# A kernel of three blocks with its whole order written as a list: a new list, filler products early in it, and one reciprocal for both softmaxes

## The chip, the core and the metric

The kernel runs on one core of a Trainium2 chip. The metric is the time of one execution on the device in microseconds. The profile of one execution shows the engines of the core: PE (TensorE, its weight loads as PEld), DVE (VectorE), ACT (ScalarE), POOL (GpSimd) and SP (SyncE), which issues the DMAs.

## The reference, cut to what matters

Attention with a band and a pooled part, then a convolution block on its result, then a mixer with two low-rank factors and two more products. q, k and v are float32; all weights are float64.

```python
def _attn_ref(q, k, v):                       # 4 batches, 8 heads, 576 tokens, 64 channels
    a = exp(s - max(s)); a = a / (sum(a) + 1e-9)          # both softmaxes
    q_d, k_d, v_d = means over 4 neighbouring tokens
    out_up = repeat(sm_attn(q_d, k_d, v_d), 4)            # 144 x 144 scores a head
    mask = |i - j| < 4                                    # the local part
    return out_up + attn_local @ v
def _moe_ref(x, w_in, conv_w, w_out):         # 512 -> 1024 -> 512
    h = relu(x @ w_in); conv of 3 taps over tokens; gate = sigmoid(conv_out)
    return h * gate @ w_out
def _moe2_ref(x, U, V, w_ch1, w_ch2):         # rank 32 over 576 tokens; 512 -> 2048 -> 512
    u = x + (x^T @ U @ V)^T
    return u + relu(u @ w_ch1) @ w_ch2
```

## The kernel before, in words

The order of everything is one string, SEQ, of 2671 words. A word is a step and its indices (`S.0.2`: scores of pair 0 in PSUM slot a2); the last lines of the kernel look each word up in a table and call its function, and a step's instructions go to the engines' queues in that order. Each engine works its queue in order, and semaphores hold it where data or a buffer is not there yet. So the list sets, for each engine, who stands behind whom.

Attention works on 16 pairs of heads, four to a batch. Steps of pair p, with engine and line:

- `lq`, `lw`, `lr` load q and k, the v windows, and v (SP, L273, L278, L282). `qs` sums four neighbours of q and k (DVE, L287); `qd` puts the scaled q sums into blocks (ACT, L295).
- `S` local scores: two mask products of 192 columns with `identR` as weights (L304) and 96 small matmuls (L311) on PE. `M` negative maxima (DVE, L326), `D` the shift (DVE, L333), `E` exp (ACT, L339), `R` row sums (DVE, L343).
- `Sd` pooled scores (PE, L364), `Md` maxima (DVE, L369), `Ed` three exps with sums (ACT, L376).
- `re`, `r` add eps (ACT, L348) and take the reciprocal (DVE, L352) of the 12 local sums; `rde`, `rd` do so for the three pooled sums. `n`, `nd` multiply (POOL, L357, L381; `nv`, `ndv` on DVE).
- `T`, `Td` transposes on PE (L398, L405); `c`, `cd` copy them from PSUM (ACT; `cv`, `cdv` on DVE); `V` 96 small matmuls with v (PE, L425), `Vd` the pooled ones (PE, L433), `vs` sums of v (POOL, L388, L391; `vsv` on DVE); `xd` scales (ACT, L441; `xdv` on DVE) and `x` adds into X (DVE, L452).

Weights come as 64-bit words. `wl` loads a tile (SP, L472; `lc` the conv weights); `wd.*.0` takes the upper words as float (ACT, L482); `wd.*.1` to `wd.*.3` shift and fill in the lower bits (DVE, L484, L486, L489; `cw.0` to `cw.3` do it for the conv weights); `wh` rounds to the first part (ACT, L502) and `wo` takes the rest (POOL, L505; `wO` on DVE). There are 16 tiles of group 1 and 32 of group 2.

The products work on six blocks of 384 tokens. Block 0 needs pairs 0 to 3, block 1 pairs 0 to 7. `px`, `pl` split X in two parts (ACT and POOL). `1.n.c` is the first product (PE, L618), n = 8 x block + tile of d_ff; `r1`, `c0`, `c1`, `th`, `gm`, `gh`, `gl` are ReLU, the conv taps, tanh, the gate (DVE, L656) and its two parts; `2.n.c` is the second product (L672). Then come the mixer (`mh` to `ma`), the turned result (`u`) and the products 3 (L746) and 4 (L764). `%Z` hands the PSUM slots 1 and 2 of attention to the products, `%A` and `%M` free SBUF of attention and of the mixer. `sp` are products on zeros ahead of the first data.

Of the kernel before, what the change touches and what calls it, by code (L numbers as in the profile page):

```python
# [18 lines left out]
SEQ = ("sf xz k z sp.1 uz lq.0 lr.0 lq.1 sp.0 lr.1 lq.2 lw.0 K lw.1 sp.1 lw.2 wl.1.0 lc wl.1.1 qs.0 wl.1.2 S.0.2 vs.0.0 "  # L19
# [164 lines left out]
P = 128  # L184
# [5 lines left out]
def mixer_kernel(ctx, tc, consts, qk, vw_, vr_, w1, w2, cw_, u_, v_, out):  # L190
# [57 lines left out]
    def clear():  # L248
        nc.gpsimd.memset(eps, 1e-9)
        for t in qds:  # L250
            nc.gpsimd.memset(t, 0.0)

    def spin_fill():
        t = pools["spin"] = xu.tile([P, 512], F32, name="spin", tag="xu0")
        nc.vector.memset(t, 0.0)
# [612 lines left out]
```

## Time and profile before

| what | value |
|---|---|
| time, median of 3 | 765.02 us (764.52 to 765.95) |
| the profiled execution | 764.64 us, span 762.7 us |
| busy in the span | PE 736.5, PEld 652.8, DVE 397.6, ACT 298.7, POOL 172.3 us |
| mean granted clock of PE | 0.975 of full |
| matmuls | 6634 |
| DMA | 46.72 MB read, 4.72 MB written |

The time is that of the whole execution; the span runs from the first instruction to the last. Busy times of PE are from instructions whose ends are modelled, so a busy PE is not one at its peak. The clock has two levels, 1.2 and 2.4 GHz; a mean between them is a mix in time.

### The profile page before, as it was taken

The numbers are of one execution on the slowest core, as the hardware profiler recorded it, in microseconds if no ns is written. First come the engines' busy times: TensorE is split into PE (matmuls) and PEld (weight loads), VectorE is DVE, ScalarE is ACT, GpSimd is POOL, SyncE is SP. The second block draws the span as 40 slices with busy tenths as digits, with TensorE's granted clock in tenths as the row PEclk, the third lists the DMA queues.
The fourth block names the chain that finished last, engine by engine and source line by source line (L and its number), as shares of the span: only waits on it lengthen the run. The fifth ranks groups of instructions, "written<-read, shape, count | busy, mean of one in ns | idle before, by whom it ended". The sixth has DMA issues, their size and how long they took to land.

```text
span 762.7 us, 15404 instructions
## 1 busy us (share of the span) xinstructions
PE 736.5 (97%) x6634; PEld 652.8 (86%) x6634; DVE 397.6 (52%) x661; ACT 298.7 (39%) x682; POOL 172.3 (23%) x161
## 2 busy tenths in 40 slices
PE   6997899999999999999999999999999999999998
PEld 4876788889988888888889898999899898988996
DVE  6479999775764899798986211311121131112111
ACT  5467686554754776665353111211111121111110
POOL 4355654652231546243221000000000000000000
PEclk9569999999999999999999999999999999999999
DMA  9854742211102200353240100100010010001001
GB/s 316 252 188 137 247 160 80 76 48 38 55 2 89 80 0 29 111 170 134 78 199 0 42 1 1 41 1 1 1 42 0 1 42 1 0 1 42 1 0 42
DMA packets 16388, 52.43 MB, mean 69 GB/s; under 512 B 1984, under 2 KB 2496, under 8 KB 16320
## 3 DMA queue, kind: packets, MB, share of 16 engines
q1 hardware_dynamic: 16320, 51.44, 19.8%
q8 instruction: 52, 0.85, 0.5%
q14 instruction: 16, 0.13, 0.1%
HBM read 46.72 MB, written 4.72 MB: 67 GB/s over the span
## 4 chain that ended last, share of the span: by engine, by line
PE 83%; DVE 11%; issue 2%; ACT 1%; DMA 1%; SPq 0%; POOL 0%; DVEq 0%; POOLq 0%; ACTq 0%
PE g L746 25%; PE acc L764 25%; PE g L618 10%; PE acc L672 10%; PE O L425 3%; DVE wval L486 2%; DVE wval L489 2%; PE Sd L364 2%; PE S L311 2%; PE O L433 1%; DVE g L645 1%; DVE wval L484 1%; PE Td L405 1%; DVE ss L287 1%; PE h L696 1%
## 5 line engine op out<-in xcount | busy, mean ns | idle before, releaser
L746 PE MATMUL g<-uT,w 128*128 128x384 f32 x1152 | 214.2, 338 | 0.9 <-DVE a L755 0.9
L764 PE MATMUL acc<-w,a 128*128 128x512 f32 x864 | 211.1, 395 | 0.2 <-DVE a L755 0.2
L746 PEld LDWEIGHTS g<-uT,w 128*128 128x128 f32 x1152 | 202.3, 188 | 7.2 <-DVE a L755 2.7
L764 PEld LDWEIGHTS acc<-w,a 128*128 128x128 f32 x864 | 161.1, 188 | 33.5 <-DVE a L755 0.7
L755 DVE SCALAR_TENSOR_TENSOR a<-g,a 128x384 fp32r<-128x384 f32 x96 | 53.4, 556 | 250.4 <-ACT a L751 250.2
L751 ACT ACTIVATE a<-g 128x384 fp32r<-128x384 f32 x96 | 47.1, 490 | 275.5 <-PE g L746 169.9
L618 PE MATMUL g<-xhl,w 128*128 128x386 f32 (+1 forms) x576 | 117.3, 349 | 3.0 <-POOL w L505 1.7
L672 PE MATMUL acc<-w,ghl 128*128 128x512 f32 x432 | 110.5, 398 | 0.5 <-POOL ghl L664 0.5
L618 PEld LDWEIGHTS g<-xhl,w 128*128 128x128 f32 x576 | 103.2, 193 | 8.9 <-POOL w L505 2.5
L672 PEld LDWEIGHTS acc<-w,ghl 128*128 128x128 f32 x432 | 79.7, 188 | 17.2 <-POOL ghl L664 0.9
L664 POOL TENSOR_TENSOR ghl<-ct,ghl 128x384 fp32r<-128x384 f32 x48 | 53.0, 1105 | 94.7 <-ACT ghl L661 89.1
L645 DVE SCALAR_TENSOR_TENSOR g<-h,cw,g 128x384 f32<-128x384 f32 x96 | 59.3, 619 | 27.6 <-ACT g L640 26.0
L505 POOL TENSOR_TENSOR w<-wval,w 128x512 fp32r<-128x512 f32 x31 | 42.7, 1379 | 77.5 <-ACT w L502 73.2
L502 ACT ACTIVATE w<-wval 128x512 fp32r<-128x512 f32 x48 | 30.1, 630 | 40.5 <-DVE wval L489 40.2
L486 DVE SCALAR_TENSOR_TENSOR wval<-raw,wval 128x512 uint32<-128x512 uint32 x48 | 43.1, 898 | 1.3
L489 DVE SCALAR_TENSOR_TENSOR wval<-raw,wval 128x512 uint32<-128x512 uint32 x48 | 42.5, 889 | 1.1
L425 PEld LDWEIGHTS O<-PT,vw 32*64 32x64 f32 x1536 | 27.5, 148 | 7.8 <-issue 5.7
L425 PE MATMUL O<-PT,vw 32*64 32x24 f32 x1536 | 29.4, 223 | 4.0 <-issue 3.1
L624 ACT ACTIVATE h<-g 128x386 f32<-128x386 f32 (+1 forms) x48 | 23.5, 490 | 22.4 <-PE g L618 22.0
L482 ACT ACTIVATE wval<-raw 128x512 f32<-128x512 f32 x48 | 31.1, 663 | 1.5 <-DVE w L505 1.0
L661 ACT ACTIVATE ghl<-ct 128x384 fp32r<-128x384 f32 x48 | 24.9, 521 | 14.0 <-PE acc L672 6.8
L656 DVE SCALAR_TENSOR_TENSOR ct<-g,h 128x384 f32<-128x384 f32 x48 | 26.4, 550 | 6.8 <-POOL ghl L664 3.4
(88 smaller groups left out, 641.0 us busy)
## 6 DMA issues: line engine op xcount, KB each, us to landing
raw<-in_w_dram SPq DMA_DIRECT2D x48, 512.0 KB, 5.4
qk<-in_qk_dram SPq DMA_DIRECT2D x16, 576.0 KB, 8.1
vw<-in_vw_dram SPq DMA_DIRECT2D x16, 384.0 KB, 3.5
vr<-in_vr_dram SPq DMA_DIRECT2D x16, 288.0 KB
out_dram<-u SPq DMA_DIRECT2D x17, 256.0 KB, 2.1
uvr<-in_v_dram SPq DMA_DIRECT2D x1, 576.0 KB
uvr<-in_u_dram SPq DMA_DIRECT2D x1, 320.0 KB
out_dram<-u SPq DMA_DIRECT2D x2, 128.0 KB, 2.0
```

Source lines behind the costliest of these rows:

```text
L425: nc.tensor.matmul(o[D * h:D * h + D, jh, c:c + NQ], e["vw"][32 * s:32 * s + 32, t, a], e["PT"][32 * s:32 * s + 32, t, 32 * a:32 * a + NQ] ...
L486: nc.vector.scalar_tensor_tensor(out=d, in0=lo, scalar=29, in1=d, op0=ALU.logical_shift_right, op1=ALU.bitwise_or)
L489: nc.vector.scalar_tensor_tensor(out=d, in0=hi, scalar=0x80000000, in1=d, op0=ALU.bitwise_and, op1=ALU.bitwise_or)
L505: eng.tensor_tensor(W[k][:, 1], vals.pop(k), W[k][:, 0].bitcast(F32), op=ALU.subtract)
L618: nc.tensor.matmul(gp[n][:, :wd], w[:, a, cc], xhl[g, cc][:, b, :wd], start=cc == 0 and i == 0, stop=cc == NCC - 1 and i == 2)
L645: nc.vector.scalar_tensor_tensor(out=o, in0=inner(g, hts[n], k), scalar=cw[:, k * NF + f:k * NF + f + 1], in1=o, op0=ALU.mult, op1=ALU.add)
L664: eng.tensor_tensor(ghl[n][:, 1], cts.pop(n), ghl[n][:, 0].bitcast(F32), op=ALU.subtract)
L672: nc.tensor.matmul(acc[g][c], t[:, a, c * P:(c + 1) * P], w[:, b], start=f == 0 and i == 0, stop=f == NF - 1 and i == 2)
L746: nc.tensor.matmul(gp["3", m][:, :TB], w[:, a, cc], uT[g, cc][:, b, :TB], start=cc == 0 and i == 0, stop=cc == NCC - 1 and i == 2)
L751: nc.scalar.activation(out=t[:, 0], in_=gp["3", m][:, :TB], func=AF.Relu)
L755: nc.vector.scalar_tensor_tensor(out=t[:, 1], in0=gp.pop(("3", m))[:, :TB], scalar=0.0, in1=t[:, 0].bitcast(F32), op0=ALU.max, op1=ALU.sub ...
L764: nc.tensor.matmul(acc2[g][c], t[:, a, c * P:(c + 1) * P], w[:, b], start=f == 0 and i == 0, stop=f == NF2 - 1 and i == 2)
```

## The change

Most of the diff is SEQ: the new list has 2643 words and all steps of the old one except `rde` and `rd`. Of the others some have another PSUM slot, and some went from POOL to DVE, from DVE to ACT or the other way (`wo` and `wO`, `ml` and `mL`, and so on). Three things are new in the code. `f.n` (three words: `f.9`, `f.6`, `f.1`) issues n products of the constants `identR` and `mask`, 192 columns each, into columns 320 to 511 of the PSUM tile that was last taken in an a slot; nothing reads them. `wm` runs an exp on the eps tile on ACT. The sums of both softmaxes lie in one of three fixed tiles of 15 columns, set to one at the start, and `re` and `r` work on all 15 columns and 128 partitions at once.

The heads of both lists, up to the line with the first product step `1.0.0`:

```diff
--- before.py
+++ after.py
-SEQ = ("sf xz k z sp.1 uz lq.0 lr.0 lq.1 sp.0 lr.1 lq.2 lw.0 K lw.1 sp.1 lw.2 wl.1.0 lc wl.1.1 qs.0 wl.1.2 S.0.2 vs.0.0 "
-       "qd.0 M.0 lq.3 Sd.0.1 vs.0.1 D.0 S.1.1 qs.1 E.0 lr.2 vs.1.0 Md.0 qd.1 lq.4 R.0 Ed.0 Sd.1.0 vs.1.1 M.1 lr.3 D.1 "
-       "Md.1 rde.0 re.0 E.1 r.0 rd.0 n.0 qs.2 Ed.1 nd.0 T.0.1 S.2.2 R.1 rde.1 c.0 rd.1 nd.1 Td.0.1 re.1 M.2 lq.5 qd.2 "
-       "V.0.0 r.1 D.2 cd.0 n.1 cw.0 E.2 cw.1 T.1.1 cw.2 cw.3 lw.3 Vd.0 wd.1.0.0 R.2 Td.1.2 c.1 wd.1.0.1 wl.1.3 wd.1.0.2 "
-       "Sd.2.0 xd.0 cd.1 x.0 V.1.1 re.2 wd.1.1.0 Md.2 px.0.0 wl.1.4 wd.1.1.1 Vd.1 Ed.2 wd.1.1.2 lw.4 r.2 pl.0.0 S.3.2 "
-       "qs.3 xd.1 n.2 rde.2 wd.1.2.0 x.1 lq.6 vs.2.0 T.2.1 qd.3 wl.1.5 M.3 px.0.1 Sd.3.0 D.3 vs.2.1 rd.2 E.3 S.4.0 cv.2 "
-       "nd.2 lr.4 Md.3 vs.3.0 V.2.2 R.3 Ed.3 M.4 D.4 vs.3.1 Td.2.1 qs.4 lw.5 rde.3 pl.0.1 re.3 lr.5 E.4 cd.2 rd.3 lq.7 "
-       "r.3 nd.3 qd.4 Vd.2 qs.5 Sd.4.0 n.3 xd.2 x.2 qd.5 T.3.1 Td.3.1 wd.1.2.1 c.3 S.5.0 wd.1.1.3 px.0.2 cd.3 Md.4 "
-       "pl.0.2 V.3.2 wh.1.1 R.4 lq.8 wd.1.2.2 Ed.4 wd.1.0.3 Vd.3 lw.6 M.5 wo.1.1 xd.3 Sd.5.0 D.5 re.4 rde.4 wh.1.0 x.3 "
-       "E.5 wo.1.0 r.4 %Z rd.4 px.0.3 Md.5 R.5 Ed.5 nd.4 1.0.0 qs.6 1.0.1 n.4 1.0.2 wd.1.3.0 vsv.4.0 T.4.0 Td.4.0 re.5 "
...
+SEQ = ("sf xz k z lq.0 uz wm lw.0 sp.1 lr.0 lq.1 lw.1 lr.1 sp.0 K lq.2 lw.2 lc wl.1.0 sp.1 wl.1.1 qs.0 wl.1.2 S.0.2 qd.0 "
+       "vs.0.0 Sd.0.1 M.0 lq.3 D.0 vs.0.1 Md.0 E.0 f.9 S.1.2 lr.2 R.0 Ed.0 qs.1 re.0 vs.1.0 r.0 qd.1 lq.4 M.1 f.6 Sd.1.1 "
+       "D.1 n.0 E.1 qs.2 nd.0 R.1 cw.0 qd.2 vsv.1.1 T.0.0 cw.1 lr.3 cw.2 Md.1 Td.0.2 wd.1.0.0 cw.3 c.0 wd.1.0.1 wl.1.3 "
+       "S.2.1 wd.1.0.2 cd.0 Ed.1 wd.1.0.3 re.1 wh.1.0 r.1 V.0.2 M.2 lq.5 n.1 wd.1.1.0 D.2 nd.1 wd.1.2.0 wl.1.4 E.2 "
+       "wl.1.5 qs.3 wo.1.0 vs.2.0 R.2 qd.3 T.1.1 lw.3 Td.1.1 c.1 wd.1.1.1 wd.1.1.2 V.1.0 wd.1.1.3 wd.1.2.1 wh.1.1 "
+       "wd.1.2.2 wd.1.2.3 wd.1.3.0 vs.3.0 wh.1.2 wl.1.6 wd.1.3.1 wd.1.3.2 Vd.0 lw.4 wd.1.3.3 wo.1.1 wh.1.3 Sd.2.1 cd.1 "
+       "wo.1.3 xd.0 Vd.1 wd.1.4.0 x.0 wl.1.7 Md.2 px.0.0 vs.2.1 S.3.2 qs.4 Ed.2 pl.0.0 lr.4 re.2 vs.3.1 xd.1 r.2 qd.4 "
+       "x.1 n.2 lr.5 Sd.3.1 lq.6 M.3 px.0.1 nd.2 D.3 E.3 wd.1.4.1 T.2.0 Md.3 pl.0.1 Td.2.2 c.2 R.3 Ed.3 wo.1.2 qs.5 "
+       "V.2.1 re.3 vs.5.0 cd.2 r.3 qd.5 wd.1.4.2 wd.1.5.0 wd.1.4.3 Vd.2 wd.1.6.0 wl.1.8 lw.5 wd.1.5.1 wh.1.4 wl.1.9 "
+       "wd.1.5.2 S.4.0 xd.2 wd.1.5.3 x.2 nd.3 wh.1.5 px.0.2 wd.1.6.1 wd.1.6.2 Sd.4.0 lq.7 M.4 n.3 D.4 wo.1.5 f.1 T.3.1 "
+       "Md.4 E.4 Td.3.2 R.4 Ed.4 vs.4.0 qs.6 S.5.0 cd.3 vs.4.1 c.3 qd.6 wd.1.6.3 lr.6 re.4 pl.0.2 wh.1.6 r.4 V.3.2 M.5 "
+       "lq.8 nd.4 D.5 E.5 Vd.3 nv.4 lw.6 Sd.5.0 R.5 wo.1.4 xd.3 x.3 vs.5.1 wd.1.7.0 %Z 1.0.0 Md.5 px.0.3 vs.6.0 wl.1.10 "
...
```

The rest of the diff:

```diff
@@ -229,6 +227,7 @@
     mask = pa.tile([P, 6, NW], F32R, name="mask")
     eps = const.tile([P, 1], F32, name="eps")
     qds = [pa.tile([P, 3, 96], F32, name=f"qd{i}") for i in range(2)]
+    sms = [pa.tile([P, 15], F32, name=f"sm{i}") for i in range(3)]
     cw = const.tile([P, NK * NF], F32, name="cw")
 
     def load_consts():
@@ -247,8 +246,14 @@
 
     def clear():
         nc.gpsimd.memset(eps, 1e-9)
+        for t in sms:
+            nc.gpsimd.memset(t, 1.0)
         for t in qds:
             nc.gpsimd.memset(t, 0.0)
+
+    def warm():
+        t = const.tile([P, 1], F32, name="warm")
+        nc.scalar.activation(out=t, in_=eps, func=AF.Exp)
 
     def spin_fill():
         t = pools["spin"] = xu.tile([P, 512], F32, name="spin", tag="xu0")
@@ -260,10 +265,18 @@
 
     st = {}
     for p in range(NPAIR):
-        st[p] = {}
+        st[p] = {"p": p}
+
+    last = {}
 
     def slot_a(n, name):
-        return (ps0 if n < 1 else pst).tile([P, 2, 512], F32, name=name, tag=f"a{n}")
+        t = last["a"] = (ps0 if n < 1 else pst).tile([P, 2, 512], F32, name=name, tag=f"a{n}")
+        return t
+
+    def beat(n):
+
+        for _ in range(n):
+            nc.tensor.matmul(last["a"][:, 1, 320:512], identR, mask.rearrange("p j x -> p (j x)"), start=True, stop=True)
 
     def slot_b(n, name):
         return (ps0 if n < 1 else pst).tile([P, 512], F32, name=name, tag=f"b{n}")
@@ -315,7 +328,7 @@
     def stats(e):
         if "sm" not in e:
             e["nm"] = pa.tile([P, 15], F32, name="nm", tag="nm", bufs=3)
-            e["sm"] = pa.tile([P, 15], F32, name="sm", tag="sm", bufs=3)
+            e["sm"] = sms[e["p"] % 3]
 
     def view(s):
         return s[:, :, :6 * NW].rearrange("p h (j x) -> p h j x", j=6)
@@ -775,10 +788,9 @@
     A, V = nc.scalar.copy, nc.vector.tensor_copy
     DV, GP = nc.vector, nc.gpsimd
     ACTS = {
-        "k": load_consts, "K": make_consts, "xz": x_pads, "z": clear, "sf": spin_fill, "sp": spin,
+        "k": load_consts, "K": make_consts, "xz": x_pads, "z": clear, "sf": spin_fill, "sp": spin, "f": beat, "wm": warm,
         "lq": load_qk, "lw": load_vw, "lr": load_vr, "qs": sums, "qd": q_blocks, "S": scores, "M": maxima,
-        "D": shifted, "E": exps, "R": rowsums, "re": lambda p: eps_add(p, P, 0, 12), "r": lambda p: recip(p, P, 0, 12),
-        "rde": lambda p: eps_add(p, 96, 12, 15), "rd": lambda p: recip(p, 96, 12, 15),
+        "D": shifted, "E": exps, "R": rowsums, "re": lambda p: eps_add(p, P, 0, 15), "r": lambda p: recip(p, P, 0, 15),
         "n": lambda p: norm(p, GP), "nv": lambda p: norm(p, DV),
         "Sd": scores_d, "Md": maxima_d, "Ed": exps_d, "nd": lambda p: norm_d(p, GP), "ndv": lambda p: norm_d(p, DV),
         "vs": vsum, "vsv": lambda p, i: vsum(p, i, DV), "T": trans, "Td": trans_d, "c": lambda p: copy_T(p, A), "cv": lambda p: copy_T(p, V),
```

## Rows read from the trace of the kernel before

**Rows 1.** Stretches of the span: busy us (instructions) of each engine, PE clock, DMA share, GB/s
```profile
0.00:51.40 51.40, 42.38 (x1081) 34.80 (x1082) 30.18 (x56) 24.76 (x79) 21.04 (x29) 0.72 0.80 259
51.40:119.90 68.50, 58.15 (x1128) 49.78 (x1127) 65.98 (x103) 50.22 (x130) 41.05 (x37) 0.93 0.53 177
119.90:250.00 130.10, 130.09 (x1888) 115.93 (x1889) 90.08 (x163) 74.94 (x184) 49.19 (x48) 1.00 0.18 56
250.00:400.00 150.00, 146.96 (x722) 128.80 (x721) 133.99 (x207) 95.16 (x184) 58.32 (x46) 1.00 0.27 98
```

**Rows 2.** Timeline of PE: start us, us, instructions [idle before <-releaser]
```profile
20.09 2.12 PE L425 MATMUL O<-PT,vw 32*64 32x24 f32 x69 [3.11 <-issue]
...
46.29 2.77 PE L425 MATMUL O<-PT,vw 32*64 32x24 f32 x96
...
98.82 1.59 PE L425 MATMUL O<-PT,vw 32*64 32x24 f32 x96
...
102.43 2.36 PE L618 MATMUL g<-xhl,w 128*128 128x386 f32 x12
...
119.91 0.43 PE L304 MATMUL S<-mask,identR 128*128 128x192 f32 x2 [1.47 <-DVE X L452]
```

**Rows 3.** DMA from 17.5 to 18 us: queue, packets, MB, share of 16 engines
```profile
q8 instruction: 1, 0.02, 12.8%
```

**Rows 4.** Timeline of DVE, first data and the step x.0
```profile
5.73 1.35 DVE L287 TENSOR_REDUCE ss<-qk 128x288 f32<-128x1152 f32 x1 [2.00 <-DMA qk<-in_qk_dram]
...
24.59 0.76 DVE L452 TENSOR_TENSOR X<-O,xd 128x576 f32<-128x576 f32 x1 [4.79 <-ACT xd L441]
```

**Rows 5.** Timeline of ACT (ScalarE), table load and conv weights
```profile
7.16 1.28 ACT L295 ACT_TABLE_LOAD   x1 [7.16 <-DVE ss L287]
...
17.41 0.22 ACT L482 ACTIVATE cw<-craw 128x24 f32<-128x24 f32 x1 [0.32 <-DMA craw<-in_cw_dram]
```

**Rows 6.** Groups by line and shape: count | busy us, mean ns | idle before, releasers
```profile
L486 DVE SCALAR_TENSOR_TENSOR wval<-raw,wval 128x512 uint32<-128x512 uint32 x48 | 43.1, 898 | 1.3
...
L489 DVE SCALAR_TENSOR_TENSOR wval<-raw,wval 128x512 uint32<-128x512 uint32 x48 | 42.5, 889 | 1.1
...
L656 DVE SCALAR_TENSOR_TENSOR ct<-g,h 128x384 f32<-128x384 f32 x48 | 26.4, 550 | 6.8 <-POOL ghl L664 3.4 <-ACT g L649 3.3
...
L484 DVE TENSOR_SCALAR wval<-wval 128x512 uint32<-128x512 uint32 x48 | 24.3, 512 | 1.5 <-ACT wval L482 1.5
...
L287 DVE TENSOR_REDUCE ss<-qk 128x288 f32<-128x1152 f32 x16 | 21.3, 1331 | 2.4 <-DMA qk<-in_qk_dram 2.0 <-PE Sd L364 0.4
...
L376 ACT ACTIVATE Pd<-Sd,nm 96x144 f32<-96x144 f32 x48 | 17.5, 369 | 2.4 <-DVE nm L369 2.3
...
L452 DVE TENSOR_TENSOR X<-O,xd 128x576 f32<-128x576 f32 x16 | 12.1, 756 | 11.7 <-ACT xd L441 11.4
L505 DVE TENSOR_TENSOR w<-wval,w 128x512 fp32r<-128x512 f32 x17 | 12.1, 711 | 1.0 <-ACT w L502 1.0
...
L369 DVE TENSOR_REDUCE nm<-Sd 96x3 f32<-96x432 f32 x16 | 9.5, 597 | 2.5 <-PE Sd L364 2.4
...
L333 DVE TENSOR_TENSOR P<-S,nm 128x384 f32<-128x384 f32 x16 | 8.9, 556 | 1.2 <-DVE nm L326 0.5
...
L343 DVE TENSOR_REDUCE sm<-P 128x12 f32<-128x384 f32 x16 | 8.6, 536 | 0.2
...
L304 PE MATMUL S<-mask,identR 128*128 128x192 f32 x32 | 8.1, 338 | 2.3 <-DVE X L452 2.3
...
L388 DVE TENSOR_TENSOR vr<-vr 72x512 f32<-72x512 f32 x5 | 5.4, 1086 | 0.0
...
L352 DVE RECIPROCAL sm<-sm 128x12 f32<-128x12 f32 x16 | 3.4, 214 | 0.0
...
L352 DVE RECIPROCAL sm<-sm 96x3 f32<-96x3 f32 x16 | 2.4, 152 | 1.2 <-ACT sm L348 1.2
...
L357 DVE TENSOR_TENSOR P<-P,sm 128x384 f32<-128x384 f32 x3 | 1.6, 549 | 0.0
```

304 rows, old and new, of the table SEQ are left out of this document.

## Prediction

> **What bounds the kernel now.** I read the stretches of the span first [rows 1], because they show where the tensor engine (PE) loses time. From 119.9 us to 250 us it is never idle at the full clock; from 250 to 400 it loses 3.0 us. Ahead of 119.9 us it is idle for 51.4 - 42.38 = 9.0 and 68.5 - 58.15 = 10.35 us, and its granted clock is 0.72 and 0.93 of full, that is, the 1.2 GHz level for about 0.28 x 51.4 x 2 = 29 and 0.07 x 68.5 x 2 = 10 us. At half speed that costs up to 19 us more. So up to 39 us lie in the first 120, and the change has to earn its gain there.
>
> Which engine rules that part? The same rows answer for DVE: it works 30.18 of the first 51.4 us (21.2 idle) and 65.98 of the next 68.5 (2.5 idle). The boundary is the end of x.3, the last step that block 0 of the products needs from attention. Thus there are two stages. In the first nobody is full and everybody waits in chains; in the second DVE is full, and PE's last wait of it, at 119.91, is for a DVE step [rows 2]. After it PE is full.
>
> The PE rows show what the first stage does [rows 2]: after part of V.0, PE stands 3.11 us on "issue", waiting for no other engine, and then V takes 2.77 us where it takes 1.59 us at the full clock. The instruction queue moved a block of 0.02 MB at 17.5 us, in the middle of that stand [rows 3], when the data loads held the DMA engines; I take it for PE's program that came late. On DVE the same event is an idle time of 4.79 us ahead of x.0 [rows 4].
>
> **Part by part.** *The list up to x.3.* Counting the words of both lists up to x.3, the new one has on DVE four more each of the decode steps 1 and 2 and five more of step 3, one more each of qs, R, r and the norm, and four small reciprocals fewer. With the rows of each [rows 6]: 4 x 0.512 + 4 x 0.898 + 5 x 0.889 = 10.1; 1.33 + 0.54 + 0.21 + 0.55 = 2.6; less 4 x 0.152 = 0.6: 12.1 us more. (The weight tiles decoded by then go from two to seven.) DVE's work up to x.3 becomes 30.2 + 12.1 = 42.3 us.
>
> When is x.3 done? I add the idle time that I cannot see filled. DVE gets its first data at 5.73 us [rows 4]; nearly all time before is idle, 4.8 us. Decoding cannot start until the conv weights and the first weight tile have landed; the conv weights came at 17.4 us [rows 5], and ScalarE decodes in order. The new list asks for them one 512 KB tile earlier, but for the first weight tile, which is needed next, one small load later, so I leave 17.4. From 5.7 to there the new list offers DVE three qs at 1.33, two each of M, D, R and Md at about 0.56, and about 1.1 us of small steps [rows 6], 9.6 us in all: 2.1 us idle. Then decode steps stand between the dependent ones, and I allow 1 us a pair for what is not covered (x.0 waits behind cd.1 and three hi-parts on ScalarE), 4 us. So 42.3 + 4.8 + 2.1 + 4 = 53.2 us, against 51.4 before. Bounds: 49 with no waits for pairs, 58 if PE at half clock paces the pairs again (V at 2.77 us, and so with its other small matmuls, is what made the old chain).
>
> *From x.3 to the point where PE is full.* I compare equal PE work. Before, that point is step S.10 at 119.9. The new list has the same PE work ahead of step 1.8.0 (15 matmuls of the first product more, 12 of which take 2.36 us [rows 2], and the fillers; V at 1.59 us and five smaller steps of one pair fewer; I set the rest at 0.5 us less). DVE has less to do by then: one D, Md, R and x (0.556 + 0.597 + 0.536 + 0.756), two v sums and two low parts that went to POOL (2 x 1.086 + 2 x 0.711) and nine small reciprocals (9 x 0.152) are gone, 7.4 us; one gate, one decode step 1, one step 2 and one norm are added, 2.5 us [rows 6]. Net 4.9 us less: 30.18 + 65.98 - 4.9 = 91.3 us. Between x.3 and 1.8.0 that leaves 49 us of DVE work. At the old idle rate of 2.5 in 66 it would idle 1.9 us; since the new order runs PE and DVE side by side at nearly one rate, each will wait for the other now and then, and I take 4 (1.9 to 8). So 1.8.0 comes at 53.2 + 49 + 4 = 106.2, where the old list would stand at 119.4: 13.2 us gained.
>
> *After it.* The new list brings the rest of attention forward (x.12 and x.15 stand before fewer products), so DVE stays nearly full where it had 90.1 of 130.1 us [rows 1]. PE is no longer alone in setting the pace; I give back 3 us (0 to 8). The 3.0 us of PE gaps at 250 to 400 can go or double (3 either way); I leave them. The last steps are the same.
>
> *One reciprocal.* For each pair a DVE instruction of 0.152 us goes (counted above), and one of two small ScalarE additions. In exchange r.p waits for Ed.p too. Behind it on DVE stand M, D and decode steps of the next pair, and E of that pair waits for those. The old small reciprocal waited for the same Ed through its addition, 1.2 us in all sixteen [rows 6], so I put it at nothing and keep the other end as a rival. The fixed tiles add three small memsets on POOL ahead of its first data; nothing.
>
> *Filler products.* 16 matmuls of the form of S's mask product, 0.338 us each by its row [rows 6]: 5.4 us at most. Nine stand where S.1 waits for D.0 to leave its PSUM slot, six ahead of Sd.1.1, which waits for qd.1. I count them as hidden; if the cover is gone, the 5.4 us delay M.1 and its chain, within the bounds above.
>
> *The table load.* ScalarE loads its table for 1.28 us at 7.16 [rows 5], between qs.0 and qd.0, with all of Sd.0, Md.0 and Ed.0 behind. The new activation on eps takes it to a time when nothing is there. Gain 0 to 1.3 us, inside the 2.1 us above.
>
> *Loads.* Ten weight tiles instead of six are asked for ahead of x.3, 2.1 MB on 51.4 us at 259 GB/s (13.3 MB) [rows 1]. The share of 0.80 would go to about 0.93 at equal time. They are behind the pairs' loads on SP; a late tile holds ScalarE, and DVE behind it, in the first stage.
>
> *The program's arrival.* Before V.0's stand PE had run 348 matmuls (6 fillers, S.0, S.1 and S.2 at 98, two Sd, one T, one Td, 27 of V.0). In the new list the 348th is the twelfth of V.0, but V.0 comes behind wd.1.0.0 on ScalarE and not right after S.2, so the block has time to arrive: the 3.1 us go into the 2.1 and 4 us above and not on top. The Trainium skill ("Runtime: NRT & Kernel Launch", section "Instruction fetch mechanics") says that the next 16 KiB block is fetched while the current one runs, and that dispatch is slower than the fill, so that fetching stays hidden. By it there is no such wait to remove, and the sum would be 3.1 us worse, 757.5, inside the forecast's own span. The trace does not agree: the 3.11 us stand on "issue" with the block moving in it.
>
> Sum: 13.2 - 3 = 10.2 us. The profiled execution took 764.64 us (span 762.7 and 1.9 around it), 0.4 under the median of 765.02; I predict 764.6 - 10.2 = 754.4.
>
> **Rivals.** (a) *PE's clock still paces the start, or the weight tiles come late.* For it: the old stage had 0.72 of the clock although PE was busy for 42.38 of 51.4 us in it [rows 1], and DMA stood at 0.80. Against: the added decode work needs no PE. x.3 at 58 us and 8 instead of 4 us of waits leave 764.6 - (13.2 - 4.8 - 4 - 3) = 763.2; the usual case of it, 760 to 763. The Trainium skill ("TensorE: Matmul & The Clock Gate", Part 1) says that the point where the clock changes moves from run to run of one kernel, which would undo fillers that were fitted to one trace. No trace here shows it; the three times before lie within 1.4 us, so it can hardly be worth more. (b) *Better than that:* x.3 at 49, old idle rate, nothing given back: 764.6 - (13.2 + 4.2 + 2.1) = 745.1. It needs the first stage to run without chains. (c) *No change:* the gain is real at 106 us and is lost again by 400, where DVE is at 134 of 150 us [rows 1]. Against: DVE idles 40 us between 119.9 and 250, so there is room. 765. (d) *Slower:* the joined reciprocal. r.p holds DVE until Ed.p is done, in a stage where DVE sets the pace. Three exps are 3 x 0.369 = 1.1 us [rows 6]; exposed in all pairs that is 17.7 us, against 10.2 gained: 772.1. It decides from 0.64 us a pair on. Against: the 1.2 us in all that the old one waited, and decode steps between Ed and r in the new list.
>
> **Chances.** Forecast (748 to 760) 0.57; (a) 0.15; (b) 0.10; (c) 0.06; (d) 0.12. The range 746 to 763 takes in (a) and half of (b). Three runs differ by 1.4 us, so 0.2% (1.5 us) is about what a measurement can tell from no change: faster 0.82, same 0.06, slower 0.12.
>
> **What would show it.** x.3 on DVE at 51 to 56 us with about 42 us of DVE work ahead; no stand of 3 us on "issue" in V.0; DVE at 95% from there; PE free of waits from about 106 us; waits of the reciprocal on ScalarE of a few us in all. The forecast fails if x.3 comes after 60 us, if PE keeps waiting for DVE between 110 and 170, or if new PE gaps of more than 3 us appear after 250.

## The result, and the profile after

The kernel before took 765.49 us (median of four, 764.52 to 769.50), the changed one 755.35 us (754.93 to 755.94): ratio 0.9858, with a 95% interval of 0.9822 to 0.9894. The forecast was 754.4 us. The profiled execution after took 755.43 us (span 753.7), 9.2 less than that of before. In the changed file every line of the kernel's functions stands 13 further down than the one of before (a few at the top differ): V is L438, x L465, the first product L631, the joined reciprocal L365, the fillers L279.

The stretches of the span after, in the columns of [rows 1], cut at the end of x.3 (60.6 us) and at product step 1.8.0 (113.7 us, the 13th of the 21 matmuls that start at 111.51):

```profile
0.00:60.60 60.60, 46.27 (x1097) 37.96 (x1098) 46.15 (x68) 31.32 (x88) 33.39 (x42) 0.66 0.78 259
60.60:113.70 53.10, 52.76 (x1021) 46.57 (x1020) 50.76 (x78) 40.76 (x103) 35.19 (x32) 0.97 0.49 166
113.70:250.00 136.30, 136.30 (x2020) 121.88 (x2019) 104.17 (x179) 83.95 (x201) 48.73 (x46) 1.00 0.21 67
250.00:400.00 150.00, 148.16 (x735) 131.22 (x735) 127.95 (x199) 90.69 (x175) 50.41 (x42) 1.00 0.25 92
```

DVE works 46.15 of the first 60.6 us and idles 14.45; before it worked 30.18 of 51.4 and idled 21.2 [rows 1]. The first stage is longer by 9.2 us, and DVE does 16 us more in it: seven weight tiles are decoded there instead of two. From x.3 on PE loses 0.3 us in 53 instead of 10.35 in 68.5, and after 250 us it idles 1.84 us instead of 3.04. The clock of the first stage did not rise (0.66 of full against 0.72).

PE's timeline after shows the places that [rows 2] shows of before:

```profile
13.90 0.25 PE L279 MATMUL S<-mask,identR 128*128 128x192 f32 x1 [1.13 <-issue]
...
22.04 2.54 PE L438 MATMUL O<-PT,vw 32*64 32x24 f32 x84 [2.20 <-issue]
...
29.74 1.91 PE L438 MATMUL O<-PT,vw 32*64 32x24 f32 x62 [2.18 <-issue]
...
51.93 0.53 PE L279 MATMUL S<-mask,identR 128*128 128x192 f32 x1 [3.10 <-DVE P L346]
...
55.52 2.77 PE L438 MATMUL O<-PT,vw 32*64 32x24 f32 x96
...
76.52 0.47 PE L317 MATMUL S<-mask,identR 128*128 128x192 f32 x2 [0.32 <-DVE X L465]
...
111.51 3.98 PE L631 MATMUL g<-xhl,w 128*128 128x386 f32 x21
```

Three stands on "issue", 5.5 us, take the place of one of 3.11. They come after 222, 348 and 475 matmuls, so 126 and 127 apart. Ahead of 250 us PE's last wait for DVE is at 76.5 us; before it was at 119.9. V at 55.52 still takes 2.77 us, the price of the 1.2 GHz level [rows 2].

DVE's timeline after, from its wait for the fillers to x.3:

```profile
14.19 0.56 DVE L346 TENSOR_TENSOR P<-S,nm 128x384 f32<-128x384 f32 x1 [2.28 <-PE S L279]
...
24.22 0.42 DVE L497 TENSOR_SCALAR wval<-wval 128x512 uint32<-128x512 uint32 x1
24.67 1.64 DVE L499 SCALAR_TENSOR_TENSOR wval<-raw,wval 128x512 uint32<-128x512 uint32 x1
...
27.41 0.69 DVE L499 SCALAR_TENSOR_TENSOR wval<-raw,wval 128x512 uint32<-128x512 uint32 x1
...
38.89 2.59 DVE L497 TENSOR_SCALAR wval<-wval 128x512 uint32<-128x512 uint32 x1
...
57.27 1.63 DVE L370 TENSOR_TENSOR P<-P,sm 128x384 f32<-128x384 f32 x1
...
59.84 0.76 DVE L465 TENSOR_TENSOR X<-O,xd 128x576 f32<-128x576 f32 x1 [0.48 <-ACT xd L454]
```

The same instruction takes 0.42 or 2.59 us, and 0.69 or 1.64. The groups of DVE's line and shape in the first 60.6 us give the means (count | busy us, mean ns | idle before):

```profile
L499 DVE SCALAR_TENSOR_TENSOR wval<-raw,wval 128x512 uint32<-128x512 uint32 x7 | 7.6, 1088 | 0.2
L497 DVE TENSOR_SCALAR wval<-wval 128x512 uint32<-128x512 uint32 x7 | 5.7, 821 | 1.0 <-ACT wval L495 1.0
L502 DVE SCALAR_TENSOR_TENSOR wval<-raw,wval 128x512 uint32<-128x512 uint32 x7 | 5.4, 773 | 0.2
...
L365 DVE RECIPROCAL sm<-sm 128x15 f32<-128x15 f32 x5 | 1.2, 245 | 1.9 <-ACT sm L361 1.9
```

The table load runs at once, and the conv weights land 1.4 us earlier than before [rows 5]; from ScalarE's timeline after:

```profile
0.73 1.28 ACT L256 ACT_TABLE_LOAD   x1 [0.73 <-PEq L866]
...
16.04 0.23 ACT L495 ACTIVATE cw<-craw 128x24 f32<-128x24 f32 x1 [0.73 <-DMA craw<-in_cw_dram]
```

### The profile page after: what moved, and what is told of

It is laid out like the page before. It is cut to its first block, busy times and chain, and to the rows that moved or that the text cites. A ratio compares the mean times of both kernels' runs of the same rounds, so it can differ in the third digit from the quotient of the medians.

```text
span 753.7 us, 15425 instructions
## 1 busy us (share of the span) xinstructions
PE 733.5 (97%) x6650; PEld 653.6 (87%) x6650; DVE 399.0 (53%) x647; ACT 297.2 (39%) x668; POOL 170.3 (23%) x161
## 4 chain that ended last, share of the span: by engine, by line
PE 84%; DVE 9%; DMA 3%; ACT 2%; issue 2%; SPq 0%; POOL 0%; DVEq 0%; ACTq 0%
PE g L759 26%; PE acc L777 26%; PE g L631 11%; PE acc L685 10%; PE O L438 2%; DVE wval L499 2%; DMA raw<-in_w_dram 2%; DVE wval L497 1%; PE S L324 1%; DVE wval L502 1%; DMA vr<-in_vr_dram 1%; PE Sd L377 1%; PE O L446 1%; PE ut L743 1%; DVE g L658 1%
## 5 line engine op out<-in xcount | busy, mean ns | idle before, releaser
L777 PE MATMUL acc<-w,a 128*128 128x512 f32 x864 | 208.6, 392 | 0.0
L631 PE MATMUL g<-xhl,w 128*128 128x386 f32 (+1 forms) x576 | 115.4, 347 | 1.0 <-DVE ct L669 1.0
L685 PE MATMUL acc<-w,ghl 128*128 128x512 f32 x432 | 108.3, 395 | 0.0
L631 PEld LDWEIGHTS g<-xhl,w 128*128 128x128 f32 x576 | 101.8, 191 | 6.0 <-DVE ct L669 2.3
L677 POOL TENSOR_TENSOR ghl<-ct,ghl 128x384 fp32r<-128x384 f32 x48 | 50.6, 1056 | 105.7 <-ACT ghl L674 86.1
L658 DVE SCALAR_TENSOR_TENSOR g<-h,cw,g 128x384 f32<-128x384 f32 x96 | 59.1, 619 | 27.2 <-ACT g L653 25.6
L438 PEld LDWEIGHTS O<-PT,vw 32*64 32x64 f32 x1536 | 27.9, 149 | 8.4 <-issue 7.3
L438 PE MATMUL O<-PT,vw 32*64 32x24 f32 x1536 | 29.8, 224 | 4.5 <-issue 4.4
L662 ACT ACTIVATE g<-g 128x384 f32<-128x384 f32 x48 | 22.7, 473 | 21.1 <-DVE g L658 21.0
```

The costliest lines, as they stand in the source:

```text
L438: nc.tensor.matmul(o[D * h:D * h + D, jh, c:c + NQ], e["vw"][32 * s:32 * s + 32, t, a], e["PT"][32 * s:32 * s + 32, t, 32 * a:32 * a + NQ] ...
L631: nc.tensor.matmul(gp[n][:, :wd], w[:, a, cc], xhl[g, cc][:, b, :wd], start=cc == 0 and i == 0, stop=cc == NCC - 1 and i == 2)
L658: nc.vector.scalar_tensor_tensor(out=o, in0=inner(g, hts[n], k), scalar=cw[:, k * NF + f:k * NF + f + 1], in1=o, op0=ALU.mult, op1=ALU.add)
L677: eng.tensor_tensor(ghl[n][:, 1], cts.pop(n), ghl[n][:, 0].bitcast(F32), op=ALU.subtract)
L685: nc.tensor.matmul(acc[g][c], t[:, a, c * P:(c + 1) * P], w[:, b], start=f == 0 and i == 0, stop=f == NF - 1 and i == 2)
L777: nc.tensor.matmul(acc2[g][c], t[:, a, c * P:(c + 1) * P], w[:, b], start=f == 0 and i == 0, stop=f == NF2 - 1 and i == 2)
```

## The experiments

Twelve kernels, each timed in five rounds beside the kernel before on the same chip; a ratio is to that kernel. Three questions: where in the list the gain lies, what paces the first stage before and after (DVE's work or PE's), and what the small parts are worth. A difference between two kernels is taken from their ratios, times 765 us; each ratio has an uncertainty of some 0.3%, 2 us, and a difference of two kernels with the change some 3 us.

**The new head with the old rest, and the reverse.** The cut is at step V.9.0 of the new list and step 1.10.2 of the old one, where both have done nearly the same steps. Words that come from the old list keep their two reciprocals. With NEW and OLD for the two lists of words, h1_newhead and h2_oldhead in turn:

```diff
+SEQ = NEW[:594] + [w for w in OLD if w not in NEW[:594]]
```
```diff
+SEQ = OLD[:612] + [w for w in NEW if w not in OLD[:612]]
```

> The new list up to V.9, then all that is left in the old order, with the old split reciprocals for the pairs of that part. The kernel before has done the same steps (but one product step, 0.55 us) at 136.7 us, the changed one at 132.7, so theory 1 (the first part and the rest each give about half) says 4.6 us under the kernel before: about 760.5. Theory 2, that of the prediction (all of the gain is made ahead of the stretch in which PE is full, and a little is given back after it) says 755 to 756. Theory 3 (the gain is the rest's alone) says 765.

Measured: 758.56 us (757.65 to 760.33), ratio 0.9896 [0.9875, 0.9917], 8.0 us less than before.

> The old list up to 1.10.2, with the old split reciprocals, no fillers and the table load in its old place, then all that is left in the new order. Theory 1 says 9.8 - 4.6, so about 5 us under the kernel before: 760. Theory 2 says 765, theory 3 says 755 to 756.

Measured: 764.59 us (761.88 to 767.87), ratio 0.9977 [0.9953, 1.0002], 1.8 us less, not to be told from nothing. The two add up to 9.8 of 10.9. So most of the gain goes with the head, which has `wm` in it (its price is measured below); the result lies between theories 1 and 2. With the old rest PE also waits after 250 us as it did before; from PE's timeline of h1_newhead between 250 and 400:

```profile
259.22 2.40 PE L634 MATMUL g<-xhl,w 128*128 128x388 f32 x12 [0.85 <-DVE ct L672]
...
292.58 0.74 PE L733 MATMUL mx<-Ht,Vs 128*128 128x512 f32 x2 [0.60 <-DVE Ht L721]
...
329.32 0.79 PE L634 MATMUL g<-xhl,w 128*128 128x386 f32 x3 [0.62 <-DVE ct L672]
...
369.79 2.37 PE L762 MATMUL g<-uT,w 128*128 128x384 f32 x12 [0.91 <-DVE a L771]
```

After the whole change two waits of half a microsecond or more are left there, in the same view:

```profile
258.25 1.32 PE L631 MATMUL g<-xhl,w 128*128 128x388 f32 x6 [1.01 <-DVE ct L669]
...
338.12 2.36 PE L759 MATMUL g<-uT,w 128*128 128x384 f32 x12 [0.63 <-DVE a L768]
```

The new rest of the list removes 1.2 us of PE's waits in those 150 us (3.04 to 1.84 us idle), which is of the size that h2_oldhead gave.

**The joined reciprocal, alone in the old list and taken out of the new one.**

```diff
-... Md.1 rde.0 re.0 E.1 r.0 rd.0 n.0 qs.2 Ed.1 nd.0 T.0.1 S.2.2 R.1 rde.1 c.0 rd.1 nd.1 Td.0.1 re.1 ...
+... Md.1 re.0 E.1 r.0 n.0 qs.2 Ed.1 nd.0 T.0.1 S.2.2 R.1 re.1 c.0 r.1 nd.1 Td.0.1 ...
```

> The old list with one reciprocal for both softmaxes and nothing else of the change. DVE loses 16 small reciprocals of 0.15 us, ten of them ahead of 120 us. If DVE's work sets the pace there, 1 to 2 us less: 763 to 764. If each pair now pays for the wait for Ed (1.1 us), up to 772; two pairs (10 and 13) have Ed late and their norm moved. If neither counts, 765.

Measured: 767.14 us (764.21 to 772.78), ratio 1.0005 [0.9979, 1.0031].

In s_new each `re.p` of the new list is two additions and each `r.p` two reciprocals, of 12 and of 3 columns.

> The changed kernel with the two old reciprocals and additions, side by side where the joined one stands. If DVE's and ScalarE's work sets the pace, 11 x 0.15 = 1.7 us more up to 133 us, and up to 2.4 in all: 757 to 758. If the joining is hidden, 755.4.

Measured: 756.41 us (755.85 to 756.64), ratio 0.9863 [0.9840, 0.9886], against 0.9858 of the changed kernel. Neither direction shows a price. In the old list the joined reciprocals wait 4.2 us for ScalarE's additions in all sixteen pairs (1.2 before [rows 6]), against 16 x 0.152 = 2.4 us of DVE's work that goes.

**The fillers.** f_none drops `f.9 f.6 f.1` from the new list, f_9only drops `f.6 f.1`.

> The changed kernel without the 16 filler products. Its trace shows three waits at them: D.1 waits 2.28 us for f.6, PE stands 1.13 us on issue inside f.6, and f.1 waits 3.10 us for D.4 with T.3 and V.3 behind it. If these are what the fillers do, the kernel gets 1 to 4 us faster: 752 to 754. If the fillers hold the clock up and so shorten the start, it gets 1 to 5 us slower: 756 to 760. If the start has slack for both, 755.4. The program is also 32 instructions shorter ahead of V.0, so the stand on issue moves to the 28th matmul of V.0.

Measured: 754.67 us (753.16 to 755.77), ratio 0.9859 [0.9830, 0.9888].

> The changed kernel with f.9 alone; f.6 and f.1, which hold D.1 and T.3, are out. If the waits at f.6 and f.1 cost and f.9 helps the clock, it is the fastest of the three: 752 to 754. If f.9 does nothing, it equals the kernel without fillers.

Measured: 754.52 us (752.39 to 755.37), ratio 0.9857 [0.9828, 0.9886]. In the profile of f_none x.3 begins at 58.04 us instead of 59.84 and the span ends 2.3 us earlier, but that execution is the fastest of its six; the ratios do not differ. The fillers are worth nothing that can be measured, for or against.

f_more keeps `f.9` and puts twelve products behind each of four V steps of the first stage:

```diff
-... r.1 V.0.2 M.2 ...
+... r.1 V.0.2 f.12 M.2 ...
```

> The changed kernel with f.9 kept, f.6 and f.1 out, and twelve filler products behind each V of pairs 0 to 3, where nothing but PE's own queue waits for them (48 matmuls of 192 columns, 96 instructions of program). The trace of the changed kernel shows 0.50 to 0.64 of the clock from 20 to 60 us. If fillers can hold the clock at 2.4 GHz there and the clock sets the pace of the first stage, x.3 comes 5 us or more before 60 us and the kernel takes 745 to 752. If they only add work (0.1 us each at the full clock, 0.3 at half), 5 to 14 us of it: 757 to 765. If PE's waits there take them in, 754 to 756, as with f.9 alone.

Measured: 757.85 us (756.14 to 761.12), ratio 0.9903 [0.9871, 0.9936], 3.5 us more than with `f.9` alone. The stretches of f_more, in the columns of [rows 1]:

```profile
20.00:40.00 20.00, 18.00 (x305) 16.04 (x307) 14.32 (x19) 9.72 (x26) 10.57 (x10) 0.50 0.82 258
40.00:50.00 10.00, 9.54 (x283) 8.65 (x268) 9.90 (x12) 6.46 (x19) 7.63 (x7) 0.86 0.73 240
```

For 20 us PE is 90% busy and stays at the 1.2 GHz level; then the clock rises for ten (0.86). x.3 begins at 64.44 us. More constant products bring some clock, and cost more than it gives.

**The table load.** wm_none drops `wm`, so ScalarE loads its table where it is first needed.

> The changed kernel with the table load back between qs.0 and qd.0. If the first chain sets the start, 1.3 us more: 756.7. If the landing of the conv weights (ScalarE waited for them at 16.0 us) is the gate, nothing: 755.4.

Measured: 758.83 us (757.47 to 759.41), ratio 0.9913 [0.9881, 0.9944]. f_none and f_9only ran on the same chip in turn with it, and no execution of either (752.39 to 755.77) reaches its fastest. Without `wm` the kernel takes about 4 us more, beyond either expectation. ScalarE's timeline of wm_none:

```profile
7.29 1.28 ACT L311 ACT_TABLE_LOAD   x1 [7.29 <-DVE ss L303]
8.59 0.65 ACT L311 ACTIVATE qd<-ss 64x144 f32<-64x144 f32 x2
```

The first blocks come 1.56 us later than after (qd.0 at 7.03 there), x.3 begins 1.2 us later, and PE's last wait for x ends at 77.62 us instead of 76.52. PE's stands on "issue" make 6.4 us instead of 5.5. So 1.1 to 1.6 us of it come from the first stage.

The rest is lost where PE hardly waits any more. The same wait as at 338.12 after, the last of PE, from its timeline of wm_none:

```profile
340.27 2.36 PE L762 MATMUL g<-uT,w 128*128 128x384 f32 x12 [0.62 <-DVE a L771]
```

From there to the end of the span (757.3 us) it is 417.0 us, after the whole change 415.6 (753.7 - 338.12), for the same list; the two kernels differ in the word `wm` alone. In the old rest of the list PE's last wait is another; from PE's timeline before:

```profile
374.56 2.37 PE L746 MATMUL g<-uT,w 128*128 128x384 f32 x12 [0.90 <-DVE a L755]
```

From there it is 388.1 us (762.7 - 374.56), and in h1_newhead, with the same old rest, 385.9 (755.7 - 369.79). All fourteen profiles fall in two groups by the word `wm`: with the new rest 415.3 to 415.6 us in seven kernels that have it and 417.0 in the two that do not (wm_none, h2_oldhead); with the old rest 385.9 with it and 388.0 to 388.1 in the four without. The fourth product is where they differ; its 864 matmuls in the whole execution after, in wm_none and before (count | busy us, mean ns):

```profile
L777 PE MATMUL acc<-w,a 128*128 128x512 f32 x864 | 208.6, 392 | 0.0
L780 PE MATMUL acc<-w,a 128*128 128x512 f32 x864 | 210.4, 394 | 0.0
L764 PE MATMUL acc<-w,a 128*128 128x512 f32 x864 | 211.1, 395 | 0.2 <-DVE a L755 0.2
```

The mean is 392 ns in all eight kernels with `wm` and 394 or 395 in all six without. So about 2 us of h1_newhead's 8.0 fall in the old rest, and go with `wm`. By then every kernel has long loaded its table; what is left of `wm` is one more tile, of four bytes a partition, so that other tiles may lie elsewhere. No run takes the tile without the early exp, so the cause stays open.

**More work for DVE in the first stage.** The q and k sums of pairs 1 to 5 are done twice, 5 x 1.34 = 6.7 us more, in the new list (q2_new) and in the old one (q2_old).

```diff
-        nc.vector.tensor_reduce(out=t.rearrange("p z x -> p (z x)"),
+        for _ in range(2 if 1 <= p <= 5 else 1):
+            nc.vector.tensor_reduce(out=t.rearrange("p z x -> p (z x)"),
```

> The same doubling of qs for pairs 1 to 5 in the old list: 6.7 us more of DVE work where DVE idled 21.2 of 51.4 us. If the prediction was right that idle DVE time in the first stage is there to be filled, under 2 us more: 765 to 767. If each DVE step of the chains counts, 6 us more: 771.

Measured: 766.32 us (764.42 to 769.38), ratio 1.0017 [0.9995, 1.0040], 1.3 us more than before.

> The changed kernel with qs of pairs 1 to 5 done twice (the same values again): 5 x 1.33 = 6.7 us more of DVE work ahead of x.3. If DVE sets the pace of the new start, 5 to 6.7 us more: 760 to 762. If PE's clock and program set it, DVE's idle time of 14.5 us takes it in: under 757.

Measured: 759.78 us (757.63 to 761.38), ratio 0.9926 [0.9898, 0.9953], 5.2 us more than the changed kernel. The old first stage hid DVE's work, the new one does not: that is the room that the new list filled. What is left of it (14.45 us idle after, 13.87 up to the end of x.3 in q2_new) did not take the work in. x.3 begins at 53.02 us in q2_old and at 65.61 in q2_new:

```profile
53.02 0.76 DVE L471 TENSOR_TENSOR X<-O,xd 128x576 f32<-128x576 f32 x1 [2.98 <-ACT xd L460]
```

That is DVE's timeline of q2_old: DVE still waits 2.98 us there. In q2_new x.3 waits 0.48.

**More work for PE in the first stage.** The 96 matmuls of V run twice for pairs 0 to 3.

```diff
-        for t in range(3):
+        for t in [0, 1, 2] * (2 if p < 4 else 1):
```

> The same doubling of V for pairs 0 to 3 in the old list. If PE at half clock set the pace of the old first stage, 6 to 11 us more: 771 to 776. If chains through the other engines did, under 4: 765 to 769.

Measured: 780.06 us (777.89 to 782.42), ratio 1.0195 [1.0166, 1.0224], 14.9 us more than before.

> The changed kernel with the 96 small matmuls of V done twice for pairs 0 to 3 (the same values again). V took 1.6 us at the full clock and 2.8 at half, so PE gets 6 to 11 us more ahead of the products, and 768 more instructions of program. If DVE sets the pace and PE has slack (14 us idle ahead of 60.6), under 3 us more: 755 to 758. If PE's clock and program set the pace, 6 to 12: 761 to 767.

Measured: 766.00 us (763.57 to 768.78), ratio 1.0018 [0.9999, 1.0036], 12.2 us more than the changed kernel. Four more V are 6.4 us at the full clock and 11.1 at half (1.59 and 2.77 each). Up to the end of x.3 PE is busy 7.6 us longer in the old list and 9.8 in the new one (50.00 instead of 42.38, 56.10 instead of 46.27), and its stands on "issue" grow by 8.1 and 3.8 us (3.1 to 11.2, and 5.5 to 9.3). Both kernels pay about the sum, so work and stands of PE cost in full in both first stages, and in the old one DVE's work hardly counts. V is also a link in the chain of each pair, from T to x; whether PE is full or the chain runs through it these runs do not tell apart. PE's timeline of v2_old:

```profile
22.08 3.62 PE L443 MATMUL O<-PT,vw 32*64 32x24 f32 x128 [4.51 <-issue]
28.82 1.27 PE L443 MATMUL O<-PT,vw 32*64 32x24 f32 x37 [3.12 <-issue]
...
48.30 4.56 PE L443 MATMUL O<-PT,vw 32*64 32x24 f32 x147 [2.10 <-issue]
...
64.10 1.60 PE L443 MATMUL O<-PT,vw 32*64 32x24 f32 x84 [1.50 <-issue]
```

These four stands are 11.2 us; before there was one of 3.1. They come after 348, 476, 986 and 1368 matmuls: 128, 4 x 127.5 and 3 x 127.3 apart (two short ones of 0.64 and 0.65 us come after 731 and 1241, on the same raster). So PE stands at the bounds of blocks of some 127 matmuls, with their weight loads some 255 instructions, which fits a program that PE runs through faster than it arrives.

No version beats the changed kernel by more than the measurement can tell (754.52 and 754.67 us without fillers, 755.35 with).

## Why the prediction was right, and where its steps were not

**The total and the mechanism.** 10.2 us were forecast; the medians give 10.1 and the ratio 10.9. That the new list moves work into DVE's idle time of the first stage, and gains by it, is borne out: DVE's work ahead of x.3 rose by 16 us for 9.2 us of time, DVE's room was real (q2_old: 6.7 us of work for 1.3) and takes no more (q2_new: 5.2), and the head alone gives 8.0. But about 4 of the 10.9 us go with `wm` (wm_none), which the sum had at 0 to 1.3, so the order of the list is worth some 4 us in the head and 7 in all. No run moved the decode steps alone; that what the order gives is theirs is argued from DVE's rows. That the total came out so near is luck in part, as the next steps show.

**The list up to x.3: mis-sized by 7.4 us.** x.3 was put at 53.2 with bounds of 49 to 58, and "fails if x.3 comes after 60 us" stood there; it ended at 60.6, so by its own sign this step failed. Of the two terms DVE's work was 46.15 us instead of 42.3, because decoding took 18.7 us (7.6 + 5.7 + 5.4) where the sum had 15.6 (5.5 in the stage of before and 10.1 added at the kernel's means): step 1 took 0.821 us instead of 0.512 and step 2 1.088 instead of 0.898. The one norm on DVE took 1.63 us instead of 0.55. The idle time was 14.45 instead of 10.9. D.1's wait for the fillers is in it (2.28 us), and so are the stands on "issue", behind which the chain of each pair stood. The bound of 58 had the cause right, PE at half clock, and was too near.

**From x.3 to step 1.8.0: right.** 53 us forecast, 53.1 measured, with 50.76 of DVE's work instead of 49 and 2.3 us idle instead of 4.

**The gain at 1.8.0: mis-sized, some 3 us instead of 13.2.** 7.5 us of it are x.3's lateness. The rest is an error in the comparison: the old list was said to stand at 119.4 at equal PE work, with the sixteen fillers counted as work and 15 matmuls more of the first product. By PE's rows the new list has at that point 12 more (2.2 us) and one pair's Sd, T, Td, V and Vd less (3.6 us, from start to start in the timeline before), so it has done 1.4 us less than the old list at 119.91, whose last 1.47 us were a wait. The old list had done as much at about 117, the new one at 113.7: 3.3 us.

**"I give back 3 us after it": the wrong sign.** PE won another 5.7 us by the end of the span (3.3 to 9.0 us by the profiles). Of these 1.5 are the old list's wait at 119.91, which still lay ahead of it at that point [rows 2]. 1.2 are waits that the new rest of the list removed between 250 and 400. About 2 are the faster fourth product that goes with `wm`, which no step of the prediction had. What is left, about 1 us, stays open. So the total came out right by two errors against each other: the stage where PE was not yet full gained 10 us less than the sum had it, and what follows gained 6 where the sum took 3 away.

**The program's arrival: right about the place, wrong that it goes.** The second stand comes after the 348th matmul, the twelfth of V.0, as counted. But the block did not "have time to arrive": three stands make 5.5 us for 3.1. The instruction queue in half a microsecond just ahead of the second stand (kernel after, 19 to 19.5 us):

```profile
q8 instruction: 1, 0.02, 13.5%
```

It is the size of the others (52 packets, 0.85 MB in the execution). It starts at 19.3 us, and PE goes on 2.7 us later; the other packets near a stand start at 11.1 and 27.1, ahead of 13.90 and 29.74, and before it was 17.6, ahead of 20.09 [rows 2, 3]. Between 11 and 27 us the packets come 8 us apart, while DMA is busy 92 and 87% of the first two 20 us. In v2_old the doubled V runs into four of these bounds. The rule of the Trainium skill that fetching stays hidden ("Runtime: NRT & Kernel Launch", section "Instruction fetch mechanics") fails here with 3.1, 5.5 and 11.2 us; its block of 16 KiB, 256 instructions, agrees with the 126 to 128 matmuls and weight loads between stands.

**Fillers "hidden", and the clock.** Not all were: D.1 waited 2.28 us for f.6, and f.6 1.1 us for the program. But without them the time does not change, and the clock of the first stage is 0.66 with them and 0.69 without (f_none, up to 58.8 us), where it was 0.72. No run shows that they raised the clock to any profit.

**The joined reciprocal and rival (d): nothing, as put.** 1.9 us of waits up to x.3, and no difference in j_old or s_new.

**The table load: mis-sized.** 0 to 1.3 us were given, inside another term; wm_none shows about 4, of which 1.1 to 1.6 come from the first stage, where the prediction looked for them, and the rest from PE's later products.

**"Nobody is full and everybody waits in chains":** incomplete. v2_old shows that PE's time in V counts in full in the old first stage, and q2_old that DVE's hardly does. So PE, at the 1.2 GHz level and standing on "issue", paced it, by itself or as a link of the pairs' chains; rival (a) had this. How the price splits between the clock and the program's arrival stays open: no run changed the one without the other.

**Loads:** they were not late to a price; DMA stayed at 0.78 of the first stage, not 0.93, since the stage grew.

## What to carry to other kernels

Find out which engine paces a stage by giving each one a little known work there: here 6.7 us on DVE cost 1.3, and 6.4 to 11.1 on PE cost 14.9. Then fill the idle engine with work that is due later, and price that work by the rows of the stage it moves into, beside the engines that will run there, not by its mean over the kernel. When two orders are compared at "equal work", count only work that both must do, and no wait. And look at the part that a change leaves alone: here its matmuls took another time too, and a gain of about 2 us that no step had forecast lay in it.

## What the runs showed of the hardware

**A DVE instruction can take longer while GpSimd works.** The shift that takes 0.42 us took 2.59 at 38.89 us. POOL's timeline after, at that time:

```profile
38.10 0.90 POOL L394 TENSOR_TENSOR Pd<-Pd,sm 96x432 f32<-96x432 f32 x1
38.96 1.00 POOL L620 TENSOR_TENSOR xhl<-X,xhl 128x386 fp32r<-128x386 f32 x1
39.93 1.26 POOL L518 TENSOR_TENSOR w<-wval,w 128x512 fp32r<-128x512 f32 x1
```

POOL works without a gap until 41.19 us, and the shift ends at 41.48, as if its 0.42 us had begun when POOL stopped. The Trainium skill ("GPSIMD Engine Reference", section "Specifications") says that GpSimd shares its memory interfaces with VectorE and that there is contention with VectorE instructions of two kinds, those in a two-port mode and those with two inputs in SBUF. The trace fits it, at up to 2.2 us for one instruction: of the 48 shifts of this shape after, ten took over 0.54 us, and POOL was busy for 91% of their time on average, against 10% for the other 38. Which kind the shift is no run shows. The 96 conv taps of L658 never took over 0.63 us, though POOL was busy for over 90% of 28 of them. No run here took POOL's work away, so the cause is argued from the two timelines.

**The program of PE comes in blocks, and can be late.** PE's stands on "issue" lie some 127 matmuls with their weight loads apart, and packets of the instruction queue come 2.5 to 2.8 us ahead of their ends in the kernels before and after. While the loads hold the DMA engines these packets come up to 8 us apart, and a step of many small matmuls runs dry (up to 4.5 us at a bound). No run changed the fetching alone.

**A busy PE does not mean a fast one.** In f_more it was busy 90% of 20 us, most of that with attention's small matmuls, and stayed at the 1.2 GHz level; beside the large products that follow x.3 it is at 0.97 of full.

**The same matmuls can run at two speeds at the full clock.** The fourth product's mean is 392 ns in the eight kernels with `wm` and 394 or 395 in the six without, and in each group the stretch after PE's last wait repeats within 0.3 us over kernels on three chips. So a difference of 0.4 to 0.6% there is not the noise of one execution.
